# Keys and queries of three more tiles transposed on TensorE, and scores one slot earlier, in an attention and two-MoE kernel

## The chip, the cores and the metric

One core of a Trainium2 chip runs the whole kernel. The metric is the device time of one execution in microseconds; of several runs the median counts.

## What is computed

Windowed attention with a few memory keys, then a dense feed-forward layer with two weight matrices, then a layer of eight experts of which each token takes one. Cut from the reference:

```python
# attention: batch 4, heads 8, seq 768, head_dim 64, 8 memory keys
for c in range(768 // 32):                       # chunks of 32 queries
    k_full = concat(mem_k, k[c*32-16 : c*32+40]) # 8 + up to 56 keys
    a = softmax(q_c @ k_full.T / 8)
    out[c] = a @ v_full
# dense layer: 3072 tokens, 512 -> 2048 -> 512
h = x @ w_in
x = (h * clip(h + 3, 0, 6) / 6) @ w_out
# experts: 8 of 512 -> 1024 -> 512, one per token
logits = normed(x) @ normed(expert_emb).T / tau
e = argmax(logits); g = softmax(logits)[e]
out[token] = g * (relu(x @ w1[e]) @ w2[e])
```

## The kernel before

The 3072 tokens are 24 tiles of 128. Tiles are grouped in 8 blocks: block 0 has tiles 0 to 3, block 1 tiles 4 and 5, and each of the blocks 2 to 7 three tiles (`BS`, `F0`). The program is written out by hand in the order in which it runs (`tc.manual_schedule()`, L962): on each engine instructions run in the order in which the code issues them, and each waits for what it reads or overwrites.

**Attention of a tile** is six functions, made by `stages(i)` (L978): transposes of the tile's queries and the next tile's keys (`st_t`, L232), scores and softmax numerators (`st_s`, L267), the row sums (`st_n`, L304), transposes of the probabilities (`st_pt`, L315), the product with the values (`st_av`, L326) and the transposes of the output (`st_xt`, L350), which give the inputs of the dense layer as a high and a low part (`xh`, `xl`).

`VT` (L67) divides the tiles by how keys and queries are transposed. Up to tile `VT - 1` each of them is loaded with one DMA of 256 KB (L156, L166), TensorE transposes it into a PSUM bank (tag `s`), ScalarE copies it from there (queries scaled, L255; keys L221) and VectorE copies the keys' context columns (L223 to L230). From tile `VT` on 16 DMAs of 16 KB (`load_blocks`, L138 to L147) put 32 x 32 blocks where VectorE's own transpose of blocks (L219, L257) gives the wanted layout; GpSimd copies the context columns, and the scaling moves into the exponential. A tile's loads are issued when the tile before it has been transposed, because the buffers for keys and queries are single.

**The dense layer** runs block by block. A step f of a block is 12 matmuls of the first layer (`mm1`, L423, with its gate on ScalarE and VectorE) for f + 1 and nine matmuls of the second layer (`mm2`, L482) for f, 16 steps per block. Attention of the tiles of block bl + 1 and the routing of the tiles of block bl - 1 (`r_t` to `r_gate`, L517 to L686) are put between these matmuls: `slot[f]` holds functions that run between `mm1(bl, f + 1)` and `mm2(bl, f)`, `pre_[f]` those ahead of `mm1(bl, f + 1)`. Which stage goes to which slot is in two lines (L1121, L1122):

```python
for o, f_ in zip((0, 2, 3, 4, 6, 7) if bl == 1 else (0, 1, 2, 3, 4, 5), st):
    slot.setdefault((1, 8)[a - 1] + o if bl == 1 else 5 * a + o, []).insert(0, f_)
```

So from block 2 on the three tiles have slots 0 to 5, 5 to 10 and 10 to 15. The routing has its own places: transposes `r_t` of the three tiles in slots 1 and 4 and ahead of step 7's first-layer matmuls, router products `r_l` ahead of step 4, in slot 6 and ahead of step 8 (`RT`, `RL`), the operands of the row lists (`r_sel`, L630) in slot 10 and the list matmuls (`r_list`, L645) in slot 11. In PSUM `r_t`, `r_l`, `r_list`, `st_pt` and `st_xt` share one bank (tag `att`), scores and values one pair of banks (tag `s`).

**Block 0** is different: its weights arrive as packed 64-bit words and are decoded while they are used. `load_w` (L378) issues one DMA of 512 KB per step, first for w_in (`raw_in`, L384), then for w_out (`raw_out`, L390); three buffers hold what is not yet decoded, and a load is issued when the decode of the weight three ahead of it has read its buffer (L413). `decode_w` (L393) takes three VectorE operations (L408, L409, L412), a copy on ScalarE (L417, the high part) and a subtraction on GpSimd (L418, the low part). First all first-layer matmuls of block 0 run, then its second layer (L1097 to L1103): step t does 12 matmuls, splits the gated values of step t + 2 (ScalarE L476, GpSimd L477), decodes a weight of step t + 2, and then runs a stage of tiles 4 to 6 if `side` (L1096) has one for t. All of these loads, and those of keys, queries and values, are issued by SP in program order.

The experts' part (from L1177 on) follows the last block.

Of the kernel before, what the change touches and what calls it, by code (L numbers as in the profile page):

```python
# [30 lines left out]
def attn_moe_kernel(ctx, tc, q, k, v, mem_k, mem_v, w_in, w_out, emb, tau, w1, w2, out, dbg=None):  # L31
# [13 lines left out]
    TB = 3  # L45
    BT = TB * P
    BS = [4, 2] + [TB] * ((NT - 6) // TB)
# [16 lines left out]
    HA, HB = (GS + 1) // 2, GS // 2  # L64
    EB = NB - 3

    VT = BS[0] + BS[1]  # L67
    SC = 1.0 / float(D) ** 0.5
    DVE, ACT, SP = mybir.EngineType.DVE, mybir.EngineType.Activation, mybir.EngineType.SP

# [24 lines left out]
    def bank2():  # L95
        if early["on"]:
            early["s"] += 1
            if early["s"] % 2:
                return pps.tile([P, 2, 512], F32, tag="sp", name="sp", bufs=1)
        return ps.tile([P, 2, 512], F32, tag="s", name="s2", bufs=1)  # L100

    def att(i, tag, name):
        if i < 2 or i == 3 and tag != "k" or (tag == "k" and i < 3):
            return pro.tile([P, H, D], F32, tag=tag + "p", name=name, bufs=3 if tag == "k" else 2)
        return ap.tile([P, H, D], F32, tag=tag, name=name, bufs=1)
# [32 lines left out]
    def load_blocks(t, x, b, s0):  # L138

        for r in range(2):  # L140
            for u in range(2):
                g = (2 * r + u) * 32
                for c in range(NCH):
                    nc.sync.dma_start(  # L144
                        out=t[g:g + 32].rearrange("p h d -> p (h d)").rearrange("p (j c d) -> p j c d", j=4, c=NCH)[:, :, c, :],
                        in_=x[b, r::2, s0 + c * CH:s0 + (c + 1) * CH, u * 32:(u + 1) * 32].rearrange("j t d -> t j d"),
                    )  # L147

    def load_q(i):
        b, s0 = i // TPB, (i % TPB) * P  # L150
        t = att(i, "q", "q_t")
        if i >= VT:
            load_blocks(t, q, b, s0)
# [5 lines left out]
    def load_k(i):  # L159
        b, s0 = i // TPB, (i % TPB) * P  # L160
        t = att(i, "k", "k_t")
        if i >= VT:
            load_blocks(t, k, b, s0)
# [41 lines left out]
    def put_k(i, pk):  # L205
        b, ti = i // TPB, i % TPB
        s = i % RING
        own = kt[:, :, s * NCH:(s + 1) * NCH, M + LC:M + LC + CH]
        src = own if i >= VT else pk.rearrange("p (j c s) -> p j c s", j=4, c=NCH)
        eng = nc.gpsimd if i >= VT else nc.vector  # L210
        c0 = s * NCH
        NR = RING * NCH
        if ti < RING:
# [3 lines left out]
            )  # L217
        if i >= VT:
            nc.vector.transpose(out=own, in_=pk)  # L219
# [12 lines left out]
    def st_t(ik, iq, between=None):  # L232

        flat = lambda t: t.rearrange("p h d -> p (h d)")
        s2 = bank2() if min(x for x in (ik, iq) if x is not None) < VT else None
        kk = None
# [280 lines left out]
    def r_t(bl, t, pt=None, more=None):  # L517

        if t == 0:
            blk[bl] = (small([P, BS[bl]], name="ss"), small([P, BS[bl], E], name="lg"))  # L520
        x2 = x2_t[bl, t]
        if pt is None:
            pt = bank("att", 1)
        for j in range(KD):
            nc.tensor.transpose(pt[:, j * P:(j + 1) * P], x2[:, j * P:(j + 1) * P], ident)
        if t == BS[bl] - 1 and more:
            q = [sb.tile([P, DM], BF16, tag=n, name="x2T", bufs=2) for n in ("gh", "gl")]
        else:
            q = sb.tile([P, 2, DM], BF16, tag="dec", name="x2T", bufs=2)
            q = [q[:, i, :] for i in range(2)]  # L530
        mid = late["x2"][2][:, t * DM // 2:(t + 1) * DM // 2] if bl == 0 else x2[:, XW + 1:XW + 1 + DM // 2]
        parts = q[0], mid.bitcast(BF16), q[1]
        x2T[bl, t] = parts
        if more is None:
            split3([(pt, parts)], nc.scalar)
        else:
            more.append((pt, parts))
# [25 lines left out]
    def r_ss(bl, t):  # L563
        junk = sb.tile([P, DM], F32, tag="dec", name="junk", bufs=2)
        nc.scalar.activation(out=junk, in_=x2_t[bl, t][:, 0:DM], func=AF.Square, accum_out=blk[bl][0][:, t:t + 1])
        if t == BS[bl] - 1:
            blk[bl] = (root(blk[bl][0]),) + blk[bl][1:]
# [394 lines left out]
    with tc.manual_schedule():  # L962
# [15 lines left out]
        def stages(i):  # L978
            def a():
                st_t(i + 1 if i + 1 < NT else None, i)  # L980

            def s_():
                st_s(i)

            def p_():
                st_pt(i)

            def v_():
                st_av(i)
                if i + 2 < NT:  # L990
                    load_mv(i + 2)
                    load_v(i + 2)

            def x_():
                st_xt(i)
            return [a, s_, lambda: st_n(i), p_, v_, x_]
# [11 lines left out]
        st = [stages(i) for i in range(BS[0] + BS[1] + 1)]  # L1008
# [95 lines left out]
        def spare(bl):  # L1104

            if bl == NB - 1:
                return bank2()[:, 0, :]
            if bl == 1 and "px" not in late:
                late["px"] = bank("acc", 3)
            return late["px"] if bl == 1 else None  # L1110

        for bl in range(NB):
            slot, pre_ = {}, {}
            if bl == 0:
                continue
            if bl + 1 < NB:
                if bl == 1:
                    slot[0] = [a6[5]]
                for a in range(bl == 1, TB):
                    st = stages(F0[bl + 1] + a)  # L1120
                    for o, f_ in zip((0, 2, 3, 4, 6, 7) if bl == 1 else (0, 1, 2, 3, 4, 5), st):  # L1121
                        slot.setdefault((1, 8)[a - 1] + o if bl == 1 else 5 * a + o, []).insert(0, f_)  # L1122
            if bl:
                d = 2 if bl == 1 else 0
                for t in range(BS[bl - 1]):
                    (wt, f), (wl, f2) = (RT4 if bl == 1 else RT)[t], (RL4 if bl == 1 else RL)[t]
                    (pre_, slot)[wt].setdefault(f, []).append(lambda t=t: r_t(bl - 1, t, spare(bl)))
                    (pre_, slot)[wl].setdefault(f2, []).insert(0, lambda t=t: r_l(bl - 1, t))
                    slot.setdefault((8, 8, 9, 9)[t] + d // 2, []).append(lambda t=t: r_ss(bl - 1, t))
                slot.setdefault(8 + d, []).append(lambda: r_route(bl - 1))  # L1130
                slot.setdefault(9 + d, []).append(lambda: r_rank(bl - 1))
                slot.setdefault(10 + d, []).append(lambda: r_sel(bl - 1))
                slot.setdefault(11 + d, []).append(lambda: r_list(bl - 1))
                slot.setdefault(12 + d, []).append(lambda: r_exp(bl - 1))
                slot.setdefault(12 + d, []).append(lambda: r_gate(bl - 1))
                if bl == EB + 1:
                    slot.setdefault(12, []).append(pick_first)
                    slot.setdefault(14, []).append(pick_rest)
            if bl == NB - 1:
                at_ctx.close()  # L1140
                p2["pool"] = ctx.enter_context(tc.tile_pool(name="p2", bufs=1, side="right", reuse_waits="tile"))
                for n in range(NE):
                    load_x(("E", n))
                eE = [nc.values_load(e0i[0:1, n:n + 1], engines=[SP], min_val=0, max_val=E - 1) for n in range(2)]
                todo = [(st, p, i) for p in range(4) for st in range(2) for i in range(2)]
                rws = {}

                def pre(n=1):
                    for _ in range(n):
                        if todo:  # L1150
                            st, p, i = todo.pop(0)
                            rws[st, p, i] = load_half(p, i, eE[st])

                def go(st, p, i, eng=None):
                    split_half(st, p, i, rws.pop((st, p, i)), eng)
                    pre()

                pre(RW)
                for n, f in enumerate(SP_):
                    slot.setdefault(f, []).append(lambda n=n: go(n // 2 % 2, n // 4, n % 2, nc.gpsimd if n in PG else None))  # L1160
                slot.setdefault(1, []).append(plan_const)
                slot.setdefault(13, []).append(lambda: T_x(("E", 0)))
            if bl == 1:
                evac(0)
            mm1(bl, 0)
            if bl > 1:
                evac(bl - 1)
            for f in range(KF):
                for g_ in pre_.get(f, []):
                    g_()  # L1170
                if f + 1 < KF:
                    mm1(bl, f + 1)
                for g_ in slot.get(f, []):
                    g_()
                if bl < NB - 1 or f < KF - 1:
                    mm2(bl, f)
# [75 lines left out]
        for i in range(2, len(seq)):  # L1252
            n, st = seq[i]
# [70 lines left out]
```

## Time and profile before

| what | us |
|---|---|
| median of 3 runs (lowest, highest) | 1068.89 (1067.87, 1069.15) |
| profiled execution | 1066.58 |
| its span on the engines | 1064.4 |
| TensorE matmuls busy | 1001.4 (94%) |
| VectorE, ScalarE, GpSimd busy | 529.2, 413.5, 166.9 |
| matmuls of the dense layer's first and second part (L434, L488), share of the chain that ended last | 21%, 20% |
| the same share, waiting on SP's small key and query loads (L144) | 2% |

The profile is of one execution; its times are microseconds from the span's start. "SPq" is SP's queue issuing DMAs. A row of the timeline has start, duration, engine, line, operation, output and inputs with their shapes, how many were merged, and in brackets the idle time just before it and what ended that.

### The profile page before, as it was taken

How to read it: one execution, taken by the hardware profiler on the slowest of the kernel's cores; microseconds unless marked ns; L12 is line 12 of the kernel's file. 1: busy time of each engine (PE TensorE's matmuls, PEld its weight loads, DVE VectorE, ACT ScalarE, POOL GpSimd, SP SyncE). 2: the span in 40 equal slices, each digit the busy share in tenths (PEclk: the TensorE clock that was granted, in tenths of full speed). 3: DMA queues.
4: the chain of work that ended last, by engine and by line, in shares of the span. 5: the costliest groups of instructions: out<-in, count | busy, mean ns of one | idle time of the engine just before them, and what ended most of it. 6: DMA issues, size and time to landing. Idle time of an engine off the chain costs nothing.

```text
span 1064.4 us, 23066 instructions
## 1 busy us (share of the span) xinstructions
PE 1001.4 (94%) x8206; PEld 841.6 (79%) x8206; DVE 529.2 (50%) x1169; ACT 413.5 (39%) x737; POOL 166.9 (16%) x220
## 2 busy tenths in 40 slices
PE   7798597989999999999999999998999999999994
PEld 4566475878888888888888888886888888888783
DVE  5677472554454554555555564756124433326530
ACT  5343332433323423323323324562235434336531
POOL 1133471000000000000000000043112211112210
PEclk9899898999999999999999999999999999999998
DMA  9754441123222232232232113331134514347610
GB/s 192 158 166 157 113 138 46 31 36 68 42 61 40 43 69 37 37 69 42 46 69 35 21 49 121 119 110 60 41 111 148 170 52 128 108 141 243 204 50 22
DMA packets 179421, 95.55 MB, mean 90 GB/s; under 512 B 146293, under 2 KB 154517, under 8 KB 179296
## 3 DMA queue, kind: packets, MB, share of 16 engines
q1 hardware_dynamic: 174688, 80.55, 29.2%
q0 software_dynamic: 4448, 13.42, 3.9%
q8 instruction: 66, 1.08, 0.4%
q14 instruction: 59, 0.48, 0.2%
q10 hardware_dynamic: 160, 0.02, 0.0%
HBM read 156.83 MB, written 13.38 MB: 160 GB/s over the span
## 4 chain that ended last, share of the span: by engine, by line
PE 75%; DVE 6%; issue 6%; DMA 4%; SPq 4%; ACT 3%; POOL 1%; POOLq 0%; DVEq 0%; ACTq 0%
PE h L434 21%; PE acc L488 20%; PE acc L836 11%; PE h L805 11%; SPq L144 2%; PE s L814 2%; PE s L333 2%; PE s L275 1%; SPq L178 1%; PE att L787 1%; DMA raw_out<-in_moe_w_out_dram 1%; DMA out_dram<-r,m_tid 1%; PE att L319 1%; PE att L203 1%; DMA xg<-xb,m_ix 1%
## 5 line engine op out<-in xcount | busy, mean ns | idle before, releaser
L488 PE MATMUL acc<-wo,gh 128*128 128x512 f32 x640 | 206.4, 404 | 2.4 <-DVE x L505 1.5
L434 PE MATMUL h<-xh,w_in_h 128*128 128x384 f32 (+2 forms) x512 | 175.7, 343 | 6.1 <-DVE wo L470 2.4
L434 PE MATMUL h<-xl,w_in_h 128*128 128x384 f32 (+2 forms) x512 | 173.1, 338 | 0.4 <-DVE xl L370 0.3
L434 PE MATMUL h<-xh,w_in_l 128*128 128x384 f32 (+2 forms) x512 | 172.8, 337 | 0.0
L488 PEld LDWEIGHTS acc<-wo,gh 128*128 128x128 f32 x640 | 113.2, 188 | 23.3 <-ACT x L507 2.6
L447 ACT ACTIVATE g<-h,three 128x384 f32<-128x384 f32 (+1 forms) x112 | 63.5, 567 | 171.6 <-PE h L434 169.5
L488 PE MATMUL acc<-wo,gl 128*128 128x512 f32 x320 | 126.2, 394 | 0.0
L448 DVE SCALAR_TENSOR_TENSOR g<-g,h 128x384 f32<-128x384 f32 (+1 forms) x112 | 59.7, 533 | 130.2 <-ACT g L447 130.0
L434 PEld LDWEIGHTS h<-xh,w_in_h 128*128 128x128 f32 x512 | 96.5, 188 | 15.0 <-DVE wo L470 3.9
L434 PEld LDWEIGHTS h<-xl,w_in_h 128*128 128x128 f32 x512 | 96.6, 189 | 7.3 <-DVE xl L370 1.1
L434 PEld LDWEIGHTS h<-xh,w_in_l 128*128 128x128 f32 x512 | 96.4, 188 | 3.0
L443 DVE TENSOR_TENSOR gl<-g,gh 128x384 fp32r<-128x384 f32 (+1 forms) x112 | 60.8, 543 | 63.2 <-ACT gh L442 63.2
L442 ACT CAST gh<-g 128x384 fp32r<-128x384 f32 (+1 forms) x112 | 55.8, 498 | 76.0 <-DVE g L448 76.0
L792 DVE TENSOR_TENSOR tl<-att,th 128x512 fp32r<-128x512 f32 x26 | 18.0, 692 | 115.0 <-ACT th L791 108.7
L488 PEld LDWEIGHTS acc<-wo,gl 128*128 128x128 f32 x320 | 60.1, 188 | 14.1 <-DVE gl L443 0.6
L773 POOL DMA_INDIRECT xg<-xb,m_ix x27 | 27.9, 1032 | 259.6 <-PE h L805 211.5
L836 PE MATMUL acc<-wo,th 128*128 128x512 f32 x192 | 60.6, 397 | 0.0
L808 ACT ACTIVATE hs<-h 128x512 f32<-128x512 f32 x54 | 32.2, 598 | 64.3 <-PE h L805 60.4
L791 ACT CAST th<-att 128x512 fp32r<-128x512 f32 x26 | 15.2, 586 | 107.3 <-PE acc L836 105.5
L223 POOL COPY kt<-kt 128x192 f32<-128x192 f32 x18 | 6.2, 347 | 320.3 <-DVE kt L219 320.3
L488 PE MATMUL acc<-wo,xh 128*128 128x512 f32 x96 | 35.4, 442 | 19.9 <-ACT wo L417 16.5
L836 PE MATMUL acc<-w_in_h,th 128*128 128x512 f32 x120 | 49.3, 410 | 0.0
(318 smaller groups left out, 1833.1 us busy)
## 6 DMA issues: line engine op xcount, KB each, us to landing
rw<-in_moe_w_dram SPq DMA_DIRECT2D x136, 512.0 KB
vw<-in_v_dram SPq DMA_DIRECT2D x176, 56.0 KB
raw_in<-in_moe_w_in_dram SPq DMA_DIRECT2D x16, 512.0 KB
raw_out<-in_moe_w_out_dram SPq DMA_DIRECT2D x16, 512.0 KB
xb<-x SPq DMA_DIRECT2D x20, 256.5 KB
k_t<-in_k_dram SPq DMA_DIRECT2D x288, 16.0 KB
q_t<-in_q_dram SPq DMA_DIRECT2D x288, 16.0 KB
k_t<-in_k_dram SPq DMA_DIRECT2D x6, 256.0 KB
```

The lines of the kernel that those rows point to most:

```text
L144: nc.sync.dma_start(out=t[g:g + 32].rearrange("p h d -> p (h d)").rearrange("p (j c d) -> p j c d", j=4, c=NCH)[:, :, c, :], in_=x[b, r::2 ...
L333: nc.tensor.matmul(op[c * CH:(c + 1) * CH, r, j * D:(j + 1) * D], lhsT=t[r * KW:(r + 1) * KW, j, c * CH:(c + 1) * CH], rhs=vt[r * KW:(r + ...
L434: nc.tensor.matmul(hp, lhsT=wt[:, c, f * P:(f + 1) * P], rhs=xc, start=(n == 0), stop=(n == 3 * KD - 1))
L442: nc.scalar.copy(out=gh, in_=g)
L443: nc.vector.tensor_tensor(out=gl, in0=g, in1=gh.bitcast(F32), op=ALU.subtract)
L447: nc.scalar.activation(out=g, in_=hp, func=AF.Relu, bias=three)
L448: nc.vector.scalar_tensor_tensor(out=g, in0=g, scalar=6.0, in1=hp, op0=ALU.min, op1=ALU.mult)
L488: nc.tensor.matmul(acc[bl][t], lhsT=gt[:, t * P:(t + 1) * P], rhs=wo[hl, f // 2][:, f % 2, :], start=(f == first and n == 0), stop=(f == l ...
L773: nc.gpsimd.indirect_dma_start(out=t[:, :], out_offset=None, in_=src, in_offset=bass.IndirectOffsetOnAxis(ap=ix[:, 0:1], axis=0), bounds_c ...
L805: nc.tensor.matmul(hp, lhsT=a[:, kk, :], rhs=wpart(st, hl, p, kk), start=(kk == 0 and a is th and hl == 0), stop=(kk == KD - 1 and a is tl))
L808: nc.scalar.activation(out=h_t[n][:, p, :], in_=hp_t.pop((n, p)), func=AF.Relu)
L836: nc.tensor.matmul(o, lhsT=a[:, KD + f, :], rhs=wpart(st, hl, 2 + half, kk), start=(f == 0 and c == 0), stop=(f == KE - 1 and c == 2))
```

## The change

Two edits. `VT` grows by three, so tiles 6, 7 and 8 are loaded whole and transposed on TensorE; VectorE's transposes begin with the tenth tile. And from block 2 on the first four stages of a block's second and third tile come one slot earlier (slots 4 to 7 and 9 to 12); their value products and output transposes stay in slots 9, 10 and 14, 15.

```diff
@@ -64,7 +64,7 @@
-    VT = BS[0] + BS[1]
+    VT = BS[0] + BS[1] + TB
@@ -1118,7 +1118,7 @@
                 for a in range(bl == 1, TB):
                     st = stages(F0[bl + 1] + a)
-                    for o, f_ in zip((0, 2, 3, 4, 6, 7) if bl == 1 else (0, 1, 2, 3, 4, 5), st):
+                    for o, f_ in zip((0, 2, 3, 4, 6, 7) if bl == 1 else (0, 1, 2, 3, 4, 5) if a == 0 else (-1, 0, 1, 2, 4, 5), st):
                         slot.setdefault((1, 8)[a - 1] + o if bl == 1 else 5 * a + o, []).insert(0, f_)
```

What it does to the order, at three places. The first is SP's queue in the second layer of block 0; `vw` are the value tiles. Before:

```order
L390 DMA raw_out<-in_moe_w_out_dram 128x1024 x6
L144 DMA k_t<-in_k_dram 32x4x32 x16
L144 DMA q_t<-in_q_dram 32x4x32 x16
L390 DMA raw_out<-in_moe_w_out_dram 128x1024 x6
L188 DMA vw_96<-in_mem_v_dram 8x4x64 x8
L178 DMA vw_96<-in_v_dram 56x4x64 x8
L390 DMA raw_out<-in_moe_w_out_dram 128x1024 x3
L144 DMA k_t<-in_k_dram 32x4x32 x16
L144 DMA q_t<-in_q_dram 32x4x32 x16
L390 DMA raw_out<-in_moe_w_out_dram 128x1024
```

and now:

```order
L390 DMA raw_out<-in_moe_w_out_dram 128x1024 x6
L166 DMA k_t<-in_k_dram 128x8x64
L156 DMA q_t<-in_q_dram 128x8x64
L390 DMA raw_out<-in_moe_w_out_dram 128x1024 x6
L188 DMA vw_96<-in_mem_v_dram 8x4x64 x8
L178 DMA vw_96<-in_v_dram 56x4x64 x8
L390 DMA raw_out<-in_moe_w_out_dram 128x1024 x3
L166 DMA k_t<-in_k_dram 128x8x64
L156 DMA q_t<-in_q_dram 128x8x64
L390 DMA raw_out<-in_moe_w_out_dram 128x1024
```

The four groups of 16 small loads ahead of two of the w_out loads are four single loads. The tile before (keys of tile 6, further up in the queue) changes in the same way.

The second place is VectorE around slot 10 of a block of three tiles (block 3): `kt` and `qT` are the transposed keys and queries, `xl` the low part of a tile's output, `mx` and `e` a tile's score maxima and shifted scores, `sel` the operands of the row lists, of which each tile has three. Before:

```order
L448 SCALAR_TENSOR_TENSOR g<-g,h_4631 128x384
L443 TENSOR_TENSOR gl<-g,gh 128x384
L219 STREAM_TRANSPOSE kt<-k_t 128x4x4x32
L257 STREAM_TRANSPOSE qT<-q_t 128x512
L370 TENSOR_TENSOR xl<-att,xh 128x4x128
L639 TENSOR_SCALAR sel<-io,r_part 128x128
L640 TENSOR_SCALAR sel<-io,r_dst 128x192
L641 TENSOR_SCALAR sel<-io,r_part,pid 128x128
```

and now:

```order
L448 SCALAR_TENSOR_TENSOR g<-g,h_4609 128x384
L443 TENSOR_TENSOR gl<-g,gh 128x384
L287 TENSOR_REDUCE mx<-s_4629 128x8
L292 TENSOR_TENSOR e<-s_4629,mx 128x2x4x64
L370 TENSOR_TENSOR xl<-att,xh 128x4x128
L639 TENSOR_SCALAR sel<-io,r_part 128x128
L640 TENSOR_SCALAR sel<-io,r_dst 128x192
L641 TENSOR_SCALAR sel<-io,r_part,pid 128x128
```

Ahead of the list operands now stand the maxima and the shifted scores of the third tile (instead of the transposes of its keys and queries, which have moved one slot up), and the shifted scores are followed by `xl`, which needs ScalarE's `xh`.

The third place is ScalarE in slots 5 to 8 of the same block: `x2T` and `x_...` on L543 and L547 are the parts of a router transpose in the `att` bank, `pT` the copy of the transposed probabilities out of the same bank. Before:

```order
L368 CAST xh<-att 128x4x128
L447 ACTIVATE g<-h_4345,three 128x384
L442 CAST gh<-g 128x384
L295 ACTIVATE e<-e 128x512
L543 CAST x2T<-att 128x512
L547 CAST x_3944<-att 128x512
L447 ACTIVATE g<-h_4436,three 128x384
L442 CAST gh<-g 128x384
L447 ACTIVATE g<-h_4483,three 128x384
L442 CAST gh<-g 128x384
L321 COPY pT<-att 128x512
```

and now:

```order
L295 ACTIVATE e<-e 128x512
L368 CAST xh<-att 128x4x128
L447 ACTIVATE g<-h_4320,three 128x384
L442 CAST gh<-g 128x384
L543 CAST x2T<-att 128x512
L547 CAST x_3881<-att 128x512
L447 ACTIVATE g<-h_4377,three 128x384
L442 CAST gh<-g 128x384
L321 COPY pT<-att 128x512
```

The exponential of the second tile (`e`) has moved ahead of `xh` and away from the router parts; between the third router transpose and `pT` one pair of gate operations is left where two were.

## Rows read from the trace of the kernel before

**Rows 1.** Stages: us, busy us (count) of PE, PEld, DVE, ACT, POOL; PEclk, DMA share, GB/s.

```profile
109.00:125.40 16.40, 12.56 (x115) 9.35 (x113) 8.56 (x15) 4.26 (x7) 9.71 (x10) 1.00 0.21 33
125.40:138.60 13.20, 6.34 (x77) 4.47 (x77) 6.23 (x9) 3.13 (x6) 4.00 (x4) 0.61 0.68 232
...
248.80:327.70 78.90, 78.71 (x791) 69.46 (x792) 40.60 (x98) 27.32 (x53) 3.51 (x13) 1.00 0.24 47
```

**Rows 2.** Timeline of PE, second layer of block 0: starts of single steps.

```profile
118.87 0.93 PE L488 MATMUL acc<-wo,xh 128*128 128x512 f32 x2
...
131.63 0.79 PE L488 MATMUL acc<-wo,xh 128*128 128x512 f32 x1 [9.52 <-ACT wo L417]
...
138.58 0.73 PE L488 MATMUL acc<-wo,xh 128*128 128x512 f32 x2
...
141.43 0.62 PE L488 MATMUL acc<-wo,xh 128*128 128x512 f32 x2
...
161.69 0.71 PE L488 MATMUL acc<-wo,xh 128*128 128x512 f32 x2
...
178.95 0.39 PE L434 MATMUL h<-xh,w_in_h 128*128 128x256 f32 x1
```

**Rows 3.** Timeline of SP: a whole-tile load, and the queue in block 0.

```profile
34.72 0.39 SPq L166 DMA_DIRECT2D k_t<-in_k_dram  x1
...
108.98 7.46 SPq L144 DMA_DIRECT2D k_t<-in_k_dram  x16
116.54 8.79 SPq L144 DMA_DIRECT2D q_t<-in_q_dram  x16
125.43 11.17 SPq L390 DMA_DIRECT2D raw_out<-in_moe_w_out_dram  x6
```

**Rows 4.** Timeline of DVE: the decode that waits for the late load.

```profile
128.71 0.69 DVE L408 TENSOR_SCALAR h<-raw_out 128x512 int32<-128x512 int32 x1 [10.45 <-DMA raw_out<-in_moe_w_out_dram]
```

**Rows 5.** Timeline, keys and queries on TensorE (54 us) and on VectorE (151 us).

```profile
54.08 0.60 PE L203 MATMUL s<-ident,k_t 128*128 128x128 f32 x4
...
54.52 0.60 PE L203 MATMUL s<-ident,q_t 128*128 128x128 f32 x4
...
56.76 0.18 DVE L230 COPY kt<-s 128x32 f32<-128x32 f32 x1
...
151.81 0.76 PE L275 MATMUL s<-kt,qT 64*32 64x64 f32 x52 [1.23 <-POOL kt L230]
```

**Rows 6.** Timeline of SP and DVE in block 4: loads of a tile, output scaling.

```profile
407.59 8.38 SPq L144 DMA_DIRECT2D k_t<-in_k_dram  x16
416.37 7.43 SPq L144 DMA_DIRECT2D q_t<-in_q_dram  x16
...
425.68 0.68 DVE L340 TENSOR_TENSOR xo<-s,sm 128x512 f32<-128x512 f32 x1
```

**Rows 7.** Timeline of DVE and PE in block 4: maxima, third router transposes.

```profile
435.92 0.68 DVE L287 TENSOR_REDUCE mx<-s 128x8 f32<-128x512 f32 x1
...
436.76 0.60 PE L525 MATMUL att<-ident,x 128*128 128x128 f32 x4
...
438.50 0.70 DVE L545 TENSOR_TENSOR att<-att,x2T 128x512 f32<-128x512 f32 x1 [1.17 <-ACT x2T L543]
...
439.29 0.62 PE L488 MATMUL acc<-wo,gh 128*128 128x512 f32 x2
...
439.85 0.69 DVE L549 TENSOR_TENSOR x2T<-att,x 128x512 bf16<-128x512 f32 x1 [0.65 <-ACT x L547]
```

**Rows 8.** Timeline of DVE and PE in block 4: list operands and what follows.

```profile
456.32 0.70 DVE L219 STREAM_TRANSPOSE kt<-k_t 128x512 f32<-128x512 f32 x1
...
458.12 0.23 DVE L639 TENSOR_SCALAR sel<-io,r_part 128x128 f16<-128x128 f16 x1
...
459.58 0.30 DVE L641 TENSOR_SCALAR sel<-io,r_part,pid 128x128 f16<-128x128 f16 x1
...
459.98 0.70 PE L488 MATMUL acc<-wo,gh 128*128 128x512 f32 x2
```

## The prediction

> **What bounds the kernel now.** I read the stages first, then TensorE's timeline where a stage is not full, then the SP queue, then the blocks in which TensorE never stops. The stage table shows two different regimes [rows 1]. From 248.8 us on, a block keeps TensorE busy for 78.71 of 78.90 us: there only TensorE's own work and new waits can change the time. At 109 to 138.6 us, in the second layer of the first block of tiles, it is busy for 12.56 of 16.40 and 6.34 of 13.20 us, and in the second of these stretches the granted clock is 0.61 of full speed.
>
> TensorE's timeline shows the hole [rows 2]: a step of this layer (12 matmuls) takes 2.85 us when nothing is missing (138.58 to 141.43), but between the start at 118.87 and the start at 138.58 lie 19.71 us for two steps and one tile's value products. Its matmuls stop for 9.52 us and wait for ScalarE's copy of a decoded weight; after the gap they run at about half speed, the 1.2 GHz level. The same thing comes a second time from 161.69 to 178.95.
>
> The SP queue shows why [rows 3]. 32 small loads of keys and queries are issued from 108.98 to 125.3 us, 0.43 to 0.5 us each, and the next weight load (raw_out) stands behind them until 125.43. VectorE has decoded everything it holds and sits idle for 10.45 us until that load lands at 128.71 [rows 4]. A whole-tile load, as earlier tiles use it, holds the queue for 0.39 us [rows 3]. Later blocks need no such weights from HBM, so the small loads are hidden there.
>
> **The change, part by part.** The sum is made against the profiled execution, 1066.58 us (span 1064.4 and 2.2 us around it); the median of the runs is 1068.89, that is 2.3 us more, and I add these 2.3 at the end.
>
> First edit (tiles 6 to 8 take the path of the earlier tiles). Six tile loads become one issue each instead of 16, so 32 issues ahead of either late weight become two, 0.8 us instead of 16. A weight's buffer comes free three steps (8.5 us) before its successor is needed and a load took 3.3 us to land [rows 3, 4], so both holes close. What stays in either stretch is two steps (5.7 us), the value products (64 small products; 52 of the like took 0.76, so 0.9) and some 0.4 for GpSimd's low half of the weight: 7.0 us. Saved: 19.71 - 7.0 = 12.7 and 17.26 - 7.0 = 10.3, together **23.0 us**, half-speed matmuls included. The first late load, that of tile 6's keys, has no such hole behind it and gives nothing.
>
> It adds 24 transposes on TensorE. Four start 0.44 us apart from the next four [rows 5], so six groups cost **+2.6 us**, half of it in this layer and half in the next block; nothing hides them. ScalarE gets six copies of about 0.6 us and is busy for 3.13 of 13.20 us in the hole's stretch [rows 1]; VectorE loses six transposes and gets eleven short copies; GpSimd loses those eleven. I cost these at nothing: they run under matmuls, and without that cover they would delay the first scores of a tile by up to 1 us. The scores of tile 6 wait 1.23 us for GpSimd's key copies now [rows 5]. On the other path VectorE ends its copies at 56.94, 2.0 us after the last transpose at 54.96 [rows 5], inside one step: **-1.2 us** (bounds 0 and -1.2).
>
> Does it matter that the transposes go to the busier engine? By time on TensorE alone this edit loses 2.6 us; only the queue makes it pay.
>
> Second edit (second and third tile of a block one slot earlier up to the probabilities' transposes). No TensorE work is added or removed: scores join the output transposes of the tile ahead and leave the router's products, so I count no change in matmul overhead. Three waits are new, in blocks 2 to 6.
>
> (a) The row lists. VectorE's list operands now stand behind the score maxima, the subtraction and a difference that needs ScalarE's exponential and copy first, instead of behind two transposes. Where that chain stands today, 2.58 us lie between the maximum at 435.92 and the VectorE operation after ScalarE's two at 438.50 [rows 7]. The maximum would start at 456.32, where the key transpose starts now; the difference then starts at 458.90 and the operands at 459.47 instead of 458.12 [rows 8]. They take 1.76 us (to 459.88 now), TensorE reaches the lists at the same place in its own work, so the matmuls after them start at 461.3 instead of 459.98: 1.3 us in each of four blocks and 0.9 in block 2, which lists two tiles: **+6.1 us** (bounds 0 and 6.9).
>
> (b) One bank. The transposes of the second tile's probabilities now come one matmul group, not a step, behind the router's third transposes, and both use the one att bank. The bank is read until 440.54, 3.78 us after those transposes started, and TensorE would be ready at 439.29, after 2.53 [rows 7]. The reading starts somewhat earlier than now, since the exponential is no longer ahead of it; I take a wait of 0.85 (bounds 0 and 1.25). Blocks 3 to 6 have a third tile to route: **+3.4 us**.
>
> (c) The router's second products wait some 0.25 us for the same bank, whose reader moves behind the exponential: five times, **+1.25 us** (bounds 0 and 2).
>
> The key and query loads of the second tile have one step less. They take 16.2 us to issue (407.59 to 423.85), land at most 3.3 us later, at 427.1, and VectorE would want the queries at 426.3, where the values' scaling (425.68) begins now [rows 6]: at most 0.8 us of VectorE, within its slack; counted at nothing (bounds 0 and 2 us in all).
>
> Sum: -23.0 + 2.6 - 1.2 + 6.1 + 3.4 + 1.25 = -10.9, so 1055.7 for a run like the profiled one and **1058 us** on the scale of the median.
>
> **The rivals.**
> 1. The second edit's waits are absorbed, because order is not time and VectorE or ScalarE run ahead of where I place them. For it: no block shows a TensorE wait of over 0.2 us today [rows 1]. Against it: the operations stand in line on one engine each. -23.0 + 2.6 - 1.2 = -21.6, so 1047.3. Chance 0.20.
> 2. The holes close only in part: with weights in time, GpSimd's two subtractions per step, which follow ScalarE's copies, set the pace instead of TensorE. Ten steps come after the first hole; 0.45 us each would give back 4.5 us: 1062.5. For it: the 0.4 us above. Against it: the step of 2.85 at 138.58 had the same subtractions. Chance 0.17.
> 3. Slower: what holds the weight is not the issuing but the moving of keys and queries. Then two big loads hold it as long as 32 small ones, the first edit gives back nothing, and its costs stay: 2.6 - 1.2 + 10.75 = +12.2, or 1081. It decides if a tile of 256 KB needs more than about 7 us to move, that is below 36 GB/s. Against it: from 109 to 125.4 us the DMA engines were busy for 0.21 of the time and moved 33 GB/s, right after it 232 GB/s [rows 1]. Chance 0.05. The Trainium skill speaks for this side: "DMA: Bandwidth & Descriptors", section "Issuing engines are not separate DMA queues", says that the sequencer's time to start a DMA is usually small against the DMA itself. By that rule the sum would be +12.2 instead of -10.9; the trace disagrees here, with 16 issues in 7.46 us and engines four fifths idle [rows 1, 3].
> 4. The second tile's queries land late in every block. VectorE's query transpose stops, and behind it the output scaling and the gate that TensorE's next step needs. At 2 us for each of five blocks it gives 1068; it begins to tell when a pair of loads takes over some 19 us instead of 16.2. Chance 0.08.
> That the change does not do what it says is no rival: the built order shows both edits in place.
>
> **How the numbers follow.** Forecast 0.50, rivals 0.20, 0.17, 0.05 and 0.08. Faster by over 0.2% (2.1 us, about what a measurement tells from no change): the forecast and rivals 1 and 2, and a little of 4: 0.88. Within 0.2%: most of rival 4, 0.05. Slower: rival 3 and the tail of 4, 0.07. The range: rival 1 sets its low end at 1047; its high end, 1064, takes in rival 2 and the upper bounds of (b) and (c). About 0.2 lies outside.
>
> **What would show it.** In the new profile: in the first block's second layer no wait of TensorE over 1 us and a granted clock of 1.00 throughout, with the next block's first matmul near 156 us instead of 178.95; VectorE's wait for raw_out gone. In blocks 3 to 6: about 2.4 us more per block, as waits of TensorE before the list products (VectorE's operands) and before the probabilities' transposes (the last read of the att bank). Wrong if the holes stay with two whole-tile loads ahead of raw_out (rival 3), if TensorE waits for GpSimd in every step (rival 2), if the later blocks keep their length (rival 1), or if VectorE waits for q_t (rival 4).

## The result and the profile after

The changed kernel takes 1059.55 us (median of 4 runs, 1058.37 to 1060.11) against 1068.38 us for the kernel before in the same comparison (4 runs): a ratio of 0.9918, 95% interval 0.9901 to 0.9936, 8.8 us less. The forecast was 1058. The traces put the gain at 6.9 us (spans 1057.5 and 1064.4), since the profiled execution of before was one of its quicker ones.

Stages of the changed kernel (columns as in [rows 1]), the two of the first block's second layer and then block 4:

```profile
109.00:125.40 16.40, 16.20 (x132) 12.77 (x131) 15.13 (x27) 7.38 (x13) 12.73 (x12) 1.00 0.62 193
125.40:138.60 13.20, 13.20 (x125) 10.74 (x124) 7.83 (x12) 6.01 (x11) 10.47 (x9) 1.00 0.61 191
...
388.37:470.55 82.18, 80.06 (x810) 69.21 (x810) 42.48 (x106) 28.55 (x57) 3.61 (x13) 1.00 0.23 45
```

The two stretches that were 12.56 of 16.40 and 6.34 of 13.20 us busy, the second at 0.61 of the clock [rows 1], are full now and at full clock. A block of three tiles takes 82.18 us instead of 78.9, and TensorE is busy in it for 80.06 instead of 78.7 us, with 2.12 us idle instead of 0.2.

The SP queue in that layer:

```profile
107.38 0.39 SPq L166 DMA_DIRECT2D k_t<-in_k_dram  x1
107.82 0.57 SPq L156 DMA_DIRECT2D q_t<-in_q_dram  x1
111.89 14.27 SPq L390 DMA_DIRECT2D raw_out<-in_moe_w_out_dram  x6
...
141.64 0.34 SPq L390 DMA_DIRECT2D raw_out<-in_moe_w_out_dram  x1
```

Two issues of half a microsecond stand where 32 stood [rows 3]. The next weight goes out at 111.89 instead of 125.43 us, and it is held by its buffer now, no longer by the queue (3.5 us without an issue lie ahead of it).

TensorE's timeline at the two seams, the first matmul of block 1 and the wait at the start of block 2:

```profile
156.90 0.39 PE L434 MATMUL h<-xh,w_in_h 128*128 128x256 f32 x1
...
226.43 0.73 PE L488 MATMUL acc<-wo,gh 128*128 128x512 f32 x2 [1.51 <-DVE x L505]
```

Block 1 starts at 156.90 instead of 178.95 us [rows 2]. At the start of block 2 the change is 22.3 us ahead (226.43; the same matmul stood at 248.77). At the first expert matmul it is 6.6 us ahead (702.8 against 709.4). So 15.7 us are lost again in blocks 2 to 6. TensorE's waits there (line that waits, what it waits for; us in total, times, longest):

```profile
PE att L649 <- DVE sel L640: 3.1, 5, 0.7
PE att L319 <- DVE x2T L549: 3.0, 4, 0.8
...
PE att L203 <- DVE x2T L549: 1.3, 2, 1.1
...
PE att L558 <- DVE xl L370: 0.7, 3, 0.2
PE s L275 <- DVE xo L340: 0.3, 1, 0.3
```

These five are new; they make 8.4 us. The rest of the 15.7 is TensorE at a slower pace around them: in block 4 it is busy for some 1.4 us more than a block before, with the same work. Block 2 (248 to 252 us) and block 4, all engines:

```profile
248.81 0.71 DVE L257 STREAM_TRANSPOSE qT<-q_t 128x512 f32<-128x512 f32 x1 [1.48 <-DMA k_t<-in_k_dram]
...
251.36 0.69 DVE L549 TENSOR_TENSOR x2T<-att,x 128x512 bf16<-128x512 f32 x1 [0.65 <-ACT x L547]
...
252.20 0.63 PE L203 MATMUL att<-ident,xo 128*128 128x128 f32 x4 [1.10 <-DVE x2T L549]
...
421.29 0.60 PE L525 MATMUL att<-ident,x 128*128 128x128 f32 x4
...
423.89 0.69 DVE L549 TENSOR_TENSOR x2T<-att,x 128x512 bf16<-128x512 f32 x1 [0.65 <-ACT x L547]
...
424.73 0.63 PE L319 MATMUL att<-ident,e 128*128 128x128 f32 x4 [0.75 <-DVE x2T L549]
...
442.07 0.69 DVE L287 TENSOR_REDUCE mx<-s 128x8 f32<-128x512 f32 x1
...
...
443.59 0.63 ACT L295 ACTIVATE e<-e 128x512 f32<-128x512 f32 x1 [2.35 <-DVE e L292]
444.13 0.57 ACT L368 CAST xh<-att 128x512 fp32r<-128x512 f32 x1
444.73 0.69 DVE L370 TENSOR_TENSOR xl<-att,xh 128x512 fp32r<-128x512 f32 x1 [1.17 <-ACT xh L368]
...
445.34 0.24 DVE L639 TENSOR_SCALAR sel<-io,r_part 128x128 f16<-128x128 f16 x1
...
445.82 0.26 PE L649 MATMUL att<-sel 128*128 128x192 f16 x1 [0.75 <-DVE sel L640]
...
446.38 0.24 PE L649 MATMUL att<-sel 128*128 128x192 f16 x1
...
446.95 0.24 PE L649 MATMUL att<-sel 128*128 128x192 f16 x1
```

Read from the bottom. The lists' products start 0.75 us late and then come 0.57 us apart, at the pace in which VectorE makes the operands; before, the three stood 0.18 us apart (459.37, 459.55, 459.72). Ahead of the operands on VectorE stand the maxima (442.07), the subtraction and the low half xl, which waits 1.17 us for ScalarE's exponential and copy. At 424.73 the probabilities' transposes wait for the router's last read of the att bank. At 248.81, in block 2 alone, VectorE waits 1.48 us for a late load.

### The profile page after: what moved, and what is told of

Same layout as the page of the kernel before. It is cut to its first block, busy times and chain, and to the rows that moved or that the text cites. A ratio compares the mean times of both kernels' runs of the same rounds, so it can differ in the third digit from the quotient of the medians.

```text
span 1057.5 us, 23039 instructions
## 1 busy us (share of the span) xinstructions
PE 1006.4 (95%) x8230; PEld 840.9 (80%) x8230; DVE 529.9 (50%) x1174; ACT 416.8 (39%) x743; POOL 163.6 (15%) x209
## 4 chain that ended last, share of the span: by engine, by line
PE 67%; DVE 12%; issue 7%; ACT 6%; DMA 3%; SPq 2%; POOL 1%; POOLq 0%; DVEq 0%; ACTq 0%
PE acc L488 18%; PE h L434 18%; PE acc L836 11%; PE h L805 11%; PE s L814 2%; PE s L333 1%; DVE g L448 1%; SPq L144 1%; DVE mx L287 1%; ACT g L447 1%; ACT gh L442 1%; DVE e L292 1%; PE att L787 1%; DVE dec L412 1%; PE att L319 1%
## 5 line engine op out<-in xcount | busy, mean ns | idle before, releaser
L805 PE MATMUL h<-wo,th 128*128 128x512 f32 x192 | 48.9, 397 | 0.0
```

Of the source, the lines that this page charges most:

```text
L805: nc.tensor.matmul(hp, lhsT=a[:, kk, :], rhs=wpart(st, hl, p, kk), start=(kk == 0 and a is th and hl == 0), stop=(kk == KD - 1 and a is tl))
```

## Experiments

All runs in one table. "Blocks 3 to 6" is the mean length of a block, from the start of block 3 to that of block 7 in each profile (four blocks: 315.85 us before, 328.24 with the change). Ratios are to the kernel before, timed on the same chip.

| run | median us | ratio (95%) | blocks 3 to 6, us |
|---|---|---|---|
| before | | | 78.96 |
| the whole change | 1059.55 | 0.9918 (0.9901 to 0.9936) | 82.06 |
| e1, first edit alone | 1047.23 | 0.9821 (0.9804 to 0.9837) | 79.00 |
| e2, second edit alone | 1083.41 | 1.0147 (1.0125 to 1.0170) | 82.34 |
| e3, first edit, third tile early | 1052.41 | 0.9862 (0.9843 to 0.9882) | 80.63 |
| e4, first edit, second tile early | 1050.27 | 0.9848 (0.9826 to 0.9871) | 80.42 |
| e5, change, list operands first | 1063.12 | 0.9951 (0.9933 to 0.9969) | 82.90 |
| e6, change, second tile's pT later | 1056.94 | 0.9892 (0.9870 to 0.9915) | 81.34 |
| e9, change, output transposes first | 1054.38 | 0.9879 (0.9857 to 0.9900) | 80.75 |
| e12, e6 and e9 together | 1047.81 | 0.9823 (0.9798 to 0.9848) | 79.83 |
| e7, whole loads, VectorE's path | 1044.57 | 0.9770 (0.9747 to 0.9794) | |
| e8, TensorE's path, 16 pieces a tile | 1066.53 | 0.9987 (0.9972 to 1.0002) | |
| e11, first edit for two tiles | 1049.60 | 0.9836 (0.9814 to 0.9858) | |
| e10, first edit, early writes | 1040.54 | 0.9750 (0.9730 to 0.9770) | |

**The edits apart (e1, e2).** The question: does the loss in blocks 2 to 6 belong to the second edit, or does the first bring it along?

```diff
e1:
-... else (0, 1, 2, 3, 4, 5) if a == 0 else (-1, 0, 1, 2, 4, 5), st):
+... else (0, 1, 2, 3, 4, 5), st):
e2:
-    VT = BS[0] + BS[1] + TB
+    VT = BS[0] + BS[1]
```

> First edit alone (tiles 6 to 8 on the earlier tiles' path, old slots). Theory A, read from the two traces: block 2 starts 22.3 us earlier with the change, and all of that is the first edit's; the 15.7 us lost again in blocks 2 to 6 belong to the second edit. Then 1044 to 1047 us, blocks 3 to 6 at 78.9 to 79.1 us each as before, and no wait of TensorE before the row lists or the probabilities' transposes. Rival R: the later loss comes with the first edit (transfers and buffers of the later blocks now lie elsewhere). Then about 1059.5, with blocks 3 to 6 at about 82 us.

> Second edit alone (tiles 6 to 8 by small loads, second and third tile one slot earlier). Theory A: the two holes of 19.7 and 17.3 us stay, block 2 starts at 248.8 us, blocks 2 to 6 are 3.0 to 3.3 us longer each: 1068.4 + 15.7 = 1084 us (1082 to 1086). By the sizes of the forecast, 10.75 us: 1079. Rival R (the loss comes with the first edit): 1068.

Both came out as theory A has it: 1047.23 (just outside the 1044 to 1047 named) and 1083.41 us, blocks of 79.00 and 82.34 us. The first edit alone is worth 19 us and the second alone costs 17 (the kernel before took 1066.47 us in this comparison). From the start of block 2 to that of block 7 the second edit costs the same without the first as with it: 15.5 us (408.75 in e2 against 393.25 before) and 15.7. The medians add up less well: -19.2 and +16.9 make -2.3 us, where the change has -8.8. Part of this gap is no edit's: in e2's profile the second layer of block 0 already starts 3.9 us later than in that of before (104.36 and 100.51 us), and up to there the two programs are the same. The rest stays open.

**The second edit's halves (e3, e4).**

```diff
e3:
-... if a == 0 else (-1, 0, 1, 2, 4, 5), st):
+... if a < 2 else (-1, 0, 1, 2, 4, 5), st):
e4:
-... if a == 0 else (-1, 0, 1, 2, 4, 5), st):
+... if a != 1 else (-1, 0, 1, 2, 4, 5), st):
```

> First edit, and of the second only the third tile's part. Theory A: this part puts the score maxima and the subtraction ahead of the list operands on VectorE; it costs the list wait (0.4 to 0.75 us), the lists' own slower pace (0.56 instead of 0.17 us from tile to tile, 0.8 us) and about 0.2 us of draining, about 1.5 us in each of five blocks: 7 to 7.5 us over the first edit alone, about 1052.5 us. No wait before the probabilities' transposes of the second tile. Rival: the list delay is caused by the second tile's shifted work ahead of it on VectorE: then as the first edit alone, about 1045.

> First edit, and of the second only the second tile's part. Theory A: the waits on the att bank (0.75 us before the probabilities' transposes in blocks 3 to 6, 0.24 before the router's second products, 1.1 before the output transposes in block 2 behind a late load of queries), each with 0.1 to 0.25 us of draining: about 8 us over the first edit alone, 1053 us; row lists without a wait. Rival: the bank waits need both tiles shifted (VectorE's whole line is late): then about 1045.

TensorE's waits in blocks 2 to 6 with the third tile early, apart from those that e1 has too:

```profile
PE att L649 <- DVE sel L640: 3.4, 5, 0.8
```

and with the second tile early:

```profile
PE att L319 <- DVE x2T L549: 2.9, 4, 0.8
PE att L203 <- DVE x2T L549: 1.4, 3, 0.9
...
PE att L558 <- DVE xl L370: 0.5, 2, 0.2
```

The waits split as theory A has them: the list wait with the third tile, the bank waits with the second. Against e1 a block is longer by 1.63 and by 1.42 us, 3.05 together; the whole change has 3.06. The medians, each good to about 2 us, say less: 5.2 and 3.0 us over e1, together 8.2, where the change has 12.3; the spans of the profiles say 8.0, 5.5 and 13.9. e4's median lies nearly 3 us below its forecast of 1053.

**Only VectorE's order? (e5).** A miss.

```diff
-                slot.setdefault(10 + d, []).append(lambda: r_sel(bl - 1))
+                slot.setdefault(10 + d, []).insert(0, lambda: r_sel(bl - 1))
```

> The whole change, with the list operands of a block put ahead of the third tile's score maxima on VectorE. Theory A: the list term is only VectorE's order; with it back, the list wait and the lists' slow pace go, 1.5 us in each of five blocks: 1059.5 - 7 = about 1052 us (1050 to 1053.5), and the lists' products come 0.17 us apart again; the waits on the att bank stay. Rival: the maxima, now 1.76 us later, delay the exponential and its copies, and the wait reappears at the third tile's output split or probabilities: 1057 to 1060.

It took 1063.12 us, more than the change itself. Block 4 of this run:

```profile
446.90 0.63 ACT L295 ACTIVATE e<-e 128x512 f32<-128x512 f32 x1 [4.04 <-DVE e L292]
447.43 0.57 ACT L368 CAST xh<-att 128x512 fp32r<-128x512 f32 x1
448.03 0.69 DVE L370 TENSOR_TENSOR xl<-att,xh 128x512 fp32r<-128x512 f32 x1 [1.17 <-ACT xh L368]
...
448.78 0.26 PE L649 MATMUL att<-sel 128*128 128x192 f16 x1 [2.16 <-DVE xl L370]
...
448.96 0.25 PE L649 MATMUL att<-sel 128*128 128x192 f16 x1
```

With the operands in time the products are 0.18 us apart again, but the first waits 2.16 us for xl. The lists need two things: their operands, and the att bank, which holds the output transposes until xl has read it. Moving the operands ahead pushed maxima, exponential, xh and xl 1.8 us back. The wait is 1.60 to 2.16 us in the five blocks. Block 4 is the longest, 84.22 us against 82.4 to 82.6 for blocks 3, 5 and 6: behind its wait the granted clock is 0.72 from 449 to 455 us, in this block alone. The rival had seen ScalarE's copies come late; that this strikes the lists themselves, through their bank, neither theory had named.

**Output transposes ahead of the scores (e9).** What delays both is then that the third tile's scores come first in the slot, so that ScalarE's exponential stands ahead of its copy xh.

```diff
-... .insert(0, f_)
+sl = slot.setdefault(..., []); sl.insert(len(sl) if bl > 1 and a == 2 and f_ is st[1] else 0, f_)
```

> The whole change, with the second tile's output transposes put ahead of the third tile's scores within their slot. Theory B, after the miss of the run with the list operands first: the lists' products write the att bank that the output transposes fill, and its last read (VectorE's low half) waits for ScalarE's copy, which stands behind the exponential; both VectorE's operands and that read are late because the scores come first. With the transposes first the low half is read before the maxima, the lists' wait is at most 0.3 us and their pace near 0.17 us again: 1.2 to 1.5 us less in each of five blocks, 1059.5 - 6.5 = 1053 us (1051.5 to 1054.5). Rival: the wait is the operands' alone, which still stand behind maxima and subtraction (1.5 us): then half of it stays, 1056 to 1058.

Block 4 of this run:

```profile
436.72 0.58 ACT L368 CAST xh<-att 128x512 fp32r<-128x512 f32 x1
437.34 0.69 DVE L370 TENSOR_TENSOR xl<-att,xh 128x512 fp32r<-128x512 f32 x1
438.26 0.69 DVE L287 TENSOR_REDUCE mx<-s 128x8 f32<-128x512 f32 x1
...
439.60 0.25 DVE L639 TENSOR_SCALAR sel<-io,r_part 128x128 f16<-128x128 f16 x1
...
440.52 0.26 PE L649 MATMUL att<-sel 128*128 128x192 f16 x1
...
440.70 0.25 PE L649 MATMUL att<-sel 128*128 128x192 f16 x1
...
441.20 0.24 PE L649 MATMUL att<-sel 128*128 128x192 f16 x1
```

The operands start 1.34 us after the maxima instead of 3.27, since the 1.17 us of waiting for ScalarE are gone from between them. The list wait is gone, blocks are 1.31 us shorter, and 1054.38 us lies in theory B's range. Only the third list still trails (0.50 us).

**The att bank (e6) and both together (e12).**

```diff
e6 (e12: this and the edit of e9):
-... if a == 0 else (-1, 0, 1, 2, 4, 5), st):
+... if a == 0 else (-1, 0, 1, 3, 4, 5) if a == 1 else (-1, 0, 1, 2, 4, 5), st):
```

> The whole change, with the second tile's probabilities' transposes back at their old slot. Theory A: the 0.75 us wait and its drain (0.25) in blocks 3 to 6 go, 4 us: about 1055.5 us (1054.5 to 1056.5), with the list wait unchanged. Rival: the wait only moves to the next user of the att bank (router's third products, one step later): 1059.

> The whole change with both mended: output transposes ahead of the third tile's scores, and the second tile's probabilities' transposes back at their old slot. Theory: the list term (1.4 us a block in the run with the transposes first) and the bank term (0.95 us a block in the run with the probabilities later) are independent and add up; what is left of the second edit is the router's second products (0.24 us and a drain a block) and block 2's late queries. Blocks 3 to 6 at 79.6 to 79.9 us instead of 82, and 1059.5 - 6.7 - 3.8 = 1049 us (1047.5 to 1051). Rival: the waits share one cause on VectorE, and mending one leaves less for the other: blocks at 80.5 us or more, 1053.

In e6 the wait before the probabilities' transposes is gone, but a block is only 0.72 us shorter, not 1.0, and 1056.94 us lies a little above the range. Blocks 3 to 5 gain 0.84 to 0.89 us and block 6 only 0.29. In block 6 a late load of queries stops VectorE, and the output transposes wait behind it, as they do in block 2 of the change:

```profile
571.08 0.71 DVE L257 STREAM_TRANSPOSE qT<-q_t 128x512 f32<-128x512 f32 x1 [0.69 <-DMA q_t<-in_q_dram]
...
574.47 0.63 PE L203 MATMUL att<-ident,xo 128*128 128x128 f32 x4 [0.73 <-DVE x2T L549]
```

In e12 the waits left in blocks 2 to 6, apart from those e1 has too, are:

```profile
PE att L558 <- DVE xl L370: 0.7, 3, 0.2
PE att L203 <- DVE x2T L549: 0.4, 2, 0.2
```

Blocks take 79.83 us: 2.23 us saved against 1.31 and 0.72 for the parts. The causes are separate, and 1047.81 us says that the stages still moved one slot early come out near the first edit alone once these two orders are mended. They give nothing beyond it.

**Issues, or moving, or the path? (e7, e8, e11).** e7 keeps VectorE's path and loads each of the three tiles whole (their keys and queries then lie in another order than the reference's, so its attention of these tiles is not the reference's); e8 takes TensorE's path and loads them in 16 pieces; e11 gives the first edit to tiles 6 and 7 alone.

```diff
e7:
-    VT = BS[0] + BS[1] + TB
+    VT = BS[0] + BS[1]
-        if i >= VT:
+        if i >= VT + TB:
             load_blocks(...)
e8, queries (keys alike):
+        for u in range(16 if i >= VT - TB else 0):
+            nc.sync.dma_start(out=t[:, u // 2, (u % 2) * 32:(u % 2) * 32 + 32], in_=q[b, u // 2, s0:s0 + P, (u % 2) * 32:(u % 2) * 32 + 32])
+        if i < VT - TB:
-        nc.sync.dma_start(out=t, in_=q[...])
+            nc.sync.dma_start(out=t, in_=q[...])
e11:
+    VT = BS[0] + BS[1] + 2
```

> Old slots; tiles 6 to 8 loaded whole, one issue each, but still transposed on VectorE and copied by GpSimd (their keys and queries then lie in another order than the reference's). Theory A: what held the late weights is the number of issues alone. Both holes close as with the first edit, and the 24 TensorE transposes (2.6 us) are saved against up to 1.2 us of waiting for GpSimd's key copies: 1.4 us below the first edit alone in span, about 1045 to 1047. Rival: VectorE's own transposes in the weight-decoding stretch are part of the hole: then 1050 or more, with waits for ScalarE's weight copy left.

> Old slots; tiles 6 to 8 on the path through TensorE, but each loaded in 16 pieces of 16 KB on the SP queue. Theory A: 32 issues ahead of each late weight again, 0.43 to 0.5 us each, so the holes of 19.7 and 17.3 us are back and the transposes come on top: 1066.5 + 1.4 = about 1068 us (1066 to 1069.5). Rival: the path (VectorE and GpSimd relieved) closes the holes: 1047.

> Old slots, first edit for tiles 6 and 7 alone: in the second hole 16 small issues (tile 8's keys) stay ahead of the last weight, and none in the first. Theory A: the weight is issued some 4 us later than with the first edit (at about 145.5 us instead of 141.6), which is within the slack of its buffer, so the hole stays closed or loses at most 2.5 us, and one tile's transposes (0.9 us of TensorE) are saved: 1047 us (1045.5 to 1049). Rival: any 16 issues ahead of the weight stop TensorE and lower its clock: 5 us more, 1052.

The SP queue of e8, whose lines are numbered 6 higher:

```profile
108.92 7.52 SPq L170 DMA_DIRECT2D k_t<-in_k_dram  x16
116.54 8.52 SPq L157 DMA_DIRECT2D q_t<-in_q_dram  x16
125.17 10.64 SPq L396 DMA_DIRECT2D raw_out<-in_moe_w_out_dram  x6
```

and its second stage, with e7's under it in a fence of its own:

```profile
125.40:138.60 13.20, 6.39 (x78) 4.61 (x79) 6.51 (x10) 3.38 (x6) 4.42 (x4) 0.74 0.75 241
```

```profile
125.40:138.60 13.20, 12.50 (x112) 9.80 (x95) 9.93 (x16) 5.36 (x10) 10.86 (x11) 1.00 0.67 197
```

The same bytes and the same transposes, in 16 issues instead of one (and with rows of 32 elements instead of 64), bring back the hole, the lowered clock and the time (0.9987). It is not the moving: from 109 to 125.4 us, while e8's pieces are issued, the DMA engines are busy for 0.30 of the time. The old path with single issues has neither hole nor lowered clock in this stretch, and at 1044.57 us it is even below e1, half a microsecond under its range. Its second layer takes 55.16 us and e1's 55.82, so the transposes on TensorE are no gain. What they cost in all these two runs don't show, since most of the 1.4 us between the spans (1042.2 and 1043.6) arises in block 2, at whose start e1 ran at a lowered clock. In e11 the last weight went out at 144.86 us, 3.2 us later than with the change, and TensorE waited 0.9 us for it at full clock. The median, 1049.60 us, is 0.6 above the range and midway between theory A's 1047 and its rival's 1052, so it doesn't decide. The trace does: the second layer takes 58.2 us, 2.4 more than in e1, which is within theory A's 2.5, and while the late weight is waited for the clock is 1.00 (it is lowered once, around 102 us, ahead of that). So 8.8 us of issues are mostly covered and 16 are not.

**A version that beats both (e10).** The wait at the start of block 2 is VectorE's scaling of a new output tile, whose buffer four writes of 256 KB still read. In e1:

```profile
225.66 0.69 DVE L505 TENSOR_SCALAR x<-acc 128x512 f32<-128x512 f32 x1 [2.42 <-DMA xb<-x]
```

The first block's gate and writes go two slots earlier:

```diff
-                slot.setdefault(12 + d, []).append(lambda: r_exp(bl - 1))
-                slot.setdefault(12 + d, []).append(lambda: r_gate(bl - 1))
+                slot.setdefault(12, []).append(lambda: r_exp(bl - 1))
+                slot.setdefault(12, []).append(lambda: r_gate(bl - 1))
```

> First edit alone, and the first block's gate and output writes two slots earlier in the second block (slot 12 instead of 14). Theory: the 1.2 to 2.4 us for which TensorE waits at the start of block 2 come from VectorE's scaling, which waits for a buffer that four 256 KB writes to DRAM still read; with the writes two slots (about 8 us) earlier the wait goes, and with it the stretch at 0.63 of full clock behind it: 2 to 3.3 us below the first edit alone, about 1044.5 us. Rival: the gate's values come too late on VectorE or the writes land no earlier: 1047.

The stages at the seam in e1 (a DMA packet counts in the stage in which it starts, so the DMA share can pass 1):

```profile
222.00:226.40 4.40, 2.50 (x12) 1.57 (x10) 1.41 (x4) 1.59 (x3) 0.00 (x0) 1.00 0.78 142
226.40:231.00 4.60, 4.60 (x23) 4.11 (x28) 2.18 (x4) 0.51 (x1) 0.88 (x4) 0.63 0.07 11
```

and in e10:

```profile
216.00:221.00 5.00, 5.00 (x28) 4.62 (x28) 1.38 (x3) 1.39 (x4) 0.00 (x0) 1.00 1.38 112
221.00:226.00 5.00, 5.00 (x82) 4.16 (x84) 3.36 (x6) 1.94 (x4) 0.88 (x4) 1.00 0.30 53
```

The wait and the slow stretch are gone, worth some 3.8 us by the traces (from the last matmuls of block 1 to the next scores, 222.76 to 230.94 us in e1 and 221.00 to 225.38 in e10). By the medians it is 6.7 us below e1 and 4 below its own forecast. In the profiles 1.5 us come from ahead of the edit: the second layer began at 99.2 us in this execution and at 100.7 in e1's. The rest of the surplus stays open. At 1040.54 us, 0.9750 of the kernel before, it beats both kernels.

## Why the prediction was right

| term | forecast, us | measured, us |
|---|---|---|
| first edit, all of it | -21.6 | -22.3 at the start of block 2 |
| (a) lists, five blocks | +6.1 | +8.1 (e3: 1.63 each) |
| (b), (c) att bank, blocks 3 to 6 | +4.4 | +5.7 (e4: 1.42 each) |
| block 2, apart from its lists | +0.25 | +1.75 (its 3.35 less 1.6) |
| sum | -10.9 | -6.7 |

The measured column is from the profiles. The term that was mis-sized is the second edit: I priced its waits at 10.75 us, and the blocks lose 15.7. For a run like the profiled one I had 1055.7 us, and the profiled execution of the change took 1059.21, 3.5 us more. The medians are closer (1058 and 1059.55) by luck: I added 2.3 us because the profile of before was that much quicker than its median, and the profile of the change is only 0.3 us quicker than its own.

**The first edit.** From the second layer's first matmul to block 1's first it took 78.44 us (100.51 to 178.95) and takes 55.92 (100.98 to 156.90): 22.5 less, where holes, half of the transposes and the scores' wait came to 22.9. The mechanism is shown twice, by the trace and by e7 with e8. Two of my signs fail to the letter at the very start of this layer: a wait of 1.28 us ahead of its first matmul, which stood there before as well, and a granted clock of 0.76 from 102 to 109 us, where it was 1.00 before. Small loads took 0.47 and 0.55 us an issue on average [rows 3], not 0.43 to 0.5; the sum used their total. I wrote that nothing hides the transposes. Their other half, 1.3 us in block 1, costs nothing: TensorE is busy there for 1.18 us more (64.73 against 63.55), but the block had 6.3 us of idle time and its length stays (69.5 and 69.8).

**(a) The lists.** The chain was right to 0.1 us: I placed VectorE's difference 2.58 us behind the maximum and it stands 2.66 behind it. Of the 2.0 us that were missing, 0.7 are block 2's: I took 0.9 us there because it lists two tiles, and it loses 1.6 like the others (80.39 us in e3, 78.80 in e1). In the other four I had 1.3 us. In e3 the matmuls behind the lists start 56.34 us after the start of block 3 and 56.65 after that of block 4, in e1 54.88 after both: 1.46 and 1.77 us later. In block 3 the maxima start where I had placed them (51.21 us after the block's start), in block 4 0.30 us later. The products' slower pace was in my term, which shifted the last operand and the matmuls behind it. e5 adds that my cause was half of it: the bank's last read is late for the same reason.

**(b), (c) The bank.** 0.75 and 0.24 us of waiting were forecast as 0.85 and 0.25. The excess is what TensorE loses around each wait beside the wait itself: in block 5 of e4 it falls 0.41 us behind e1 at the shorter one and 0.94 at the longer, 0.2 us more than either. That term I had at nothing.

**Block 2.** I had counted the late loads of the second tile at nothing. In block 2 VectorE waited 1.48 us for them, the router's split behind them came late, and the output transposes waited 1.10 us for its bank. That is rival 4's mechanism, in one block of five. It does not belong to block 2: it strikes block 2 again in e9 (1.29 us of VectorE), block 4 in e2 (1.12), block 6 in e6 (0.69), and none in e5 and e12.

**The rivals.** Rival 1 (waits absorbed) fell: e1 shows the 1047 us that it would have given, and the change is 12 us above it. Rival 2 (GpSimd's pace) gives back 0.9 us in two waits, not 4.5. Rival 3 (moving, not issuing) fell with e8. For it spoke the Trainium skill ("DMA: Bandwidth & Descriptors", section "Issuing engines are not separate DMA queues"), by which the time to start a DMA is usually small against the DMA itself. This case is not the usual one: 32 issues took 16 us and two take one, and that decided. Rival 4 holds for one block.

## To carry to other kernels

A step that brings no engine time can still cost: ask of each operation that moves ahead which in-order engine it now leads, and which bank its neighbours share. Count small loads ahead of a needed one by their issues, not their bytes, and see if the slack covers them (here 8.8 us mostly, 16 us not). When a stream of matmuls is fed late, price the drain and the slower pace as well as the wait; the waits listed here were 8.4 of 15.7 us.

On the shared bank the Trainium skill has advice in its page "Perfetto Trace Analysis", section "Matmuls": independent groups of matmuls should rotate through several PSUM banks, so that reading one overlaps filling the next. No run here gives these groups a second bank. The traces show what one bank costs: with att shared by outputs, probabilities, router and lists, the change has waits for its last reader of 0.2 to 1.1 us and e5 of up to 2.2, and in e12 another order leaves only five of at most 0.24.

## What was not expected of the hardware

The same short wait at the start of block 2 was followed by a lowered clock in some executions and not in others: after 1.90 us in e1 the next 4.6 us ran at 0.63, and e3, e5 and e12 had the like after 1.7 to 2.2 us, but after 2.51 us in e9 and 2.65 us in e11 it ran at 1.00. In the same way the second layer of block 0 opens with waits of 1.3 and 0.6 us in the change and before, and of these two only the change has a lowered clock behind them (0.76 from 102 to 109 us). The length of the wait alone doesn't tell the cases apart, and what does stays open.

The second layer starts at 98.3 (e9) to 104.4 us (e2) in these profiles, though no edit touches the matmuls ahead of it. The granted clock from 30 to 52 us goes with it: 1.00 in e9 and e11 (starts at 98.3 and 99.0 us), 0.92 in e6, e7 and e10 (99.2 to 100.3), 0.84 in before, the change, e1, e3 and e12 (100.5 to 101.9), 0.77 in e2, e4, e5 and e8 (100.3 to 104.4). Why it differs from one execution to the next stays open. So differences of a few microseconds between whole profiles say little here, and the length of the same stretch says more.
